# Reordering the first loads and two output steps of a windowed-attention and SwiGLU kernel

## The chip, the cores and the metric

The kernel runs on one core of a Trainium2 chip. The metric is the device time of one execution in microseconds (us). Before the change the median of three runs is 244.04 us (243.81 to 244.27). The profile is of one execution, whose span from the first to the last instruction is 240.8 us, at a mean granted tensor-engine clock of 0.998 of full speed.

## The reference

Attention with a causal window of 128 tokens and 4 "sink" tokens that every query may see, over 4 batches, 8 heads, 768 tokens and a head size of 64; its output, as 3072 tokens of 512 features, goes through a SwiGLU block with 1536 hidden features. Inputs and outputs are float32.

```python
scores = scale * np.matmul(q, k.transpose(0, 1, 3, 2))
keep = is_sink | in_window              # window: 0 <= query - key < 128
a = softmax(np.where(keep, scores, -1e9))
attn = np.matmul(a, v)                  # [B, H, S, D]
x = attn.transpose(0, 2, 1, 3).reshape(B * S, H * D)
g, val = x @ w_gate, x @ w_val
out = (g * sigmoid(g) * val) @ w_out
```

## The kernel before

The 3072 tokens are cut into 12 groups of 256 (three for each batch) for the attention, and into 8 blocks of 256 or 512 tokens (`SIZES`) for the SwiGLU block. Block 0, 1 and 2 are groups 0, 1 and 2; block 3 holds groups 3 and 4. Groups 1 and 2 get their keys and queries by `load_rows` and are transposed on TensorE (`step_T`); from group 3 on they come by `load_nat` and are transposed by a DMA (`xbar`). All loads of keys, queries, values and weights are issued by GpSimd (they cast float32 to bfloat16 on the way), in the order of the program:

```python
FCH = [2, 2, 2, 2, 4]          # chunks of the gate and value weights, in columns of 128

def load_gate(i):
    f0, n = sum(FCH[:i]) * P, FCH[i] * P
    for lst, w, nm in ((wgs, moe_w_gate, "wg"), (wvs, moe_w_val, "wv")):
        t = wpool.tile([P, DMC, n], BF16, tag=f"{nm}{i}", name=nm)
        nc.gpsimd.dma_start(t, w[:, f0:f0 + n].rearrange("(c p) f -> p c f", p=P))
        lst.append(t)
# [...]
load_rows(1)
load_v(0)
load_gate(0)
load_v(1)
load_gate(1)
load_gate(2)
nc.gpsimd.tensor_copy(out=vcf[64:128], in_=vcf[0:64])
load_gate(3)
load_rows(2)
load_v(2)
load_gate(4)
for i in range(4):
    load_out(i)
```

After these come the loads of group 3 (`load_nat(3)`, `load_v(3)`), then those of later groups. The DMA transposes are issued by SyncE, as are the stores of the output:

```python
def xbar(g):                                       # keys and queries, group 3 on
    # [...]
            nc.sync.dma_start_transpose(
                (kTs, qTs)[i][b][:, :, t0:t0 + P], nats[g][:, i, j])

def step_X(g, j, evict="v"):                       # attention output -> xT
    # [...]
    if g not in PEX:                               # PEX = (0, 1, 2, 4)
        def sp():
            nc.sync.dma_start_transpose(xTs[tb][:, :, off:off + P], xns[g, j])
        later.append(sp)
        return
    pt = bank([P, DMC, P], BF16, "px")
    for i in range(DMC):
        nc.tensor.transpose(pt[:, i], xns[g, j][:, i * P:(i + 1) * P], ident)
    # [...]  copy to xT by ScalarE ("a"), by VectorE at once ("now"), or later
```

One unit of the SwiGLU block is a `gate` (two matmul groups pg and pv, with a tanh, and two VectorE operations after them) or a `down` (12 matmuls pd, a scaling on ScalarE and a store). Attention steps are woven into the units: a gate runs them between pg and pv, a down spreads them over its matmuls. What a step leaves to VectorE or SyncE goes to `later` and is emitted by `flush`.

```python
us = [g0[0], g0[1], g0[2], g1[0], g1[1],           # units 0 to 4
      g1[2], g0[3], g1[3], g0[4], g1[4], g0[5], g1[5],   # 5 to 11
      *g2, *downs(0), *downs(1), *downs(2)]        # 12 to 17, then 18 to 23
weave(us, slots(
    (0, [K(1)]), (1, PVs(1)[:2] + [...]),
    (2, [A(step_X, 1, 0, "a"), A(step_X, 1, 1, "a")]),
    ((4, 4, 5, 5), T(2)), ((6, 7), Ss(2)), (6, [K(2)]),
    ((8, 8, 9, 9), PVs(2)), (11, [A(step_X, 2, 0, "now"), A(step_X, 2, 1, "now")]),
    # [...]  loads and DMA transposes of groups 3 to 7
    ((17, 18), Ss(3)), # [...]
    ((19, 19, 20, 20), PVs(3)), (21, Xs(3)),
    ((19, 20), Ss(4)), (19, [K(4)]),
    ((21, 21, 22, 22), PVs(4)), (22, Xs(4))))
```

`g0[i]` is the gate of block 0 that uses weight columns 2i and 2i + 1. `T` transposes keys and queries, `Ss` makes scores and their exponentials, `K` those of the sink tokens, `PVs` multiplies with the values and normalises (xn), `Xs` transposes xn into xT, the input of the gates. The units of block 3 come after unit 23.

Of the kernel before, what the change touches and what calls it, by code (L numbers as in the profile page):

```python
# [14 lines left out]
def kernel(  # L15
# [29 lines left out]
    PEX = (0, 1, 2, 4)  # L45

    VS = 72
    FCH = [2, 2, 2, 2, 4]
    FOF = [(i, f - sum(FCH[:i])) for i in range(len(FCH))
           for f in range(sum(FCH[:i]), sum(FCH[:i + 1]))]  # L50
    scale = 1.0 / float(D) ** 0.5
# [32 lines left out]
    def by_rows(src, b, w, pairs, t0):  # L84

        hs = slice(2 * pairs.start + w, 2 * pairs.stop, 2)
        return src[b, hs, t0:t0 + 256].rearrange("p (m r) d -> m p (r d)", r=4)
# [3 lines left out]
    def new_rows(g):  # L91
        rows[g] = rowp.tile([P, 2, NP2, 4 * D], BF16, tag="rows", name="rows")
        return rows[g]

    def load_rows(g, pairs=ALL, tensors=(0, 1)):
        b, c = divmod(g, GC)
        x = rows[g] if g in rows else new_rows(g)
        for i in tensors:
            for w in range(2):
                nc.gpsimd.dma_start(  # L100
                    x[64 * w:64 * (w + 1), i, pairs],
                    by_rows((k, q)[i], b, w, pairs, c * 256))
# [12 lines left out]
    def load_v(g):  # L115
        b, c = divmod(g, GC)
        va = vpool.tile([P, 2, H, VS], BF16, tag=f"va{g}", name="va")
        nc.vector.memset(va[:, :, :, D:D + 1], 1.0)
        for j in range(2):
            t0 = c * 256 + j * P  # L120
            nc.gpsimd.dma_start(  # L121
                va[:, j, :, 0:D], v[b, :, t0:t0 + P].rearrange("h p d -> p h d"))
        vas[g] = va

    wgs, wvs, wos = [], [], []

    def load_gate(i):
        f0, n = sum(FCH[:i]) * P, FCH[i] * P
        for lst, w, nm in ((wgs, moe_w_gate, "wg"), (wvs, moe_w_val, "wv")):
            t = wpool.tile([P, DMC, n], BF16, tag=f"{nm}{i}", name=nm)  # L130
            nc.gpsimd.dma_start(
                t, w[:, f0:f0 + n].rearrange("(c p) f -> p c f", p=P))
            lst.append(t)

    def load_out(i):
        n = DFC // 4
        t = wpool.tile([P, n, DM], BF16, tag=f"wo{i}", name="wo")
        nc.gpsimd.dma_start(
            t, moe_w_out[i * n * P:(i + 1) * n * P].rearrange("(c p) f -> p c f", p=P))
        wos.append(t)  # L140
# [47 lines left out]
    load_rows(1)  # L188
    load_v(0)
    load_gate(0)  # L190
    load_v(1)
    load_gate(1)
    load_gate(2)
    nc.gpsimd.tensor_copy(out=vcf[64:128], in_=vcf[0:64])
    load_gate(3)
    load_rows(2)
    load_v(2)
    load_gate(4)
    for i in range(4):
        load_out(i)  # L200

# [264 lines left out]
    def A(fn, *a):  # L466
        return lambda: fn(*a)

    def T(g):
        return [A(step_T, g, i, p2) for p2 in range(2) for i in range(2)]  # L470

    def Ss(g):
        return [A(step_S, g, p2) for p2 in range(2)]

    def PVs(g):
        return [A(step_PV, g, j, hh) for hh in range(2) for j in range(2)]

    def Xs(g):
        return [A(step_X, g, j) for j in range(2)]

    def K(g):
        return A(step_K, g)
# [109 lines left out]
    def L(*fs):  # L592
        def f():
            for x in fs:
                x()
        return f
# [2 lines left out]
        (0, [K(1)]), (1, PVs(1)[:2] + [A(step_PV, 1, 0, 1, "a"), A(step_PV, 1, 1, 1, "a"), flush]),  # L599
        (2, [A(step_X, 1, 0, "a"), A(step_X, 1, 1, "a")]),  # L600
        ((4, 4, 5, 5), T(2)), ((6, 7), Ss(2)), (6, [K(2)]),
        ((8, 8, 9, 9), PVs(2)), (11, [A(step_X, 2, 0, "now"), A(step_X, 2, 1, "now")]),
        (11, [L(A(load_nat, 4), A(load_v, 4))]),
        (12, [A(xbar, 3)]), (12, [L(A(load_nat, 5), A(load_v, 5))]),
        (15, [A(xbar, 4)]), (15, [L(A(load_nat, 6), A(load_v, 6))]),
        ((17, 18), Ss(3)), (18, [A(step_ks, 1)]), (18, [A(step_vsb, 1)]),
        (17, [A(xbar, 5)]), (17, [L(A(load_nat, 7), A(load_v, 7))]),
        ((19, 19, 20, 20), PVs(3)), (21, Xs(3)),
        ((19, 20), Ss(4)), (19, [K(4)]),
        ((21, 21, 22, 22), PVs(4)), (22, Xs(4))))  # L610

# [56 lines left out]
```

The softmax here doesn't subtract the row's maximum and nothing guards it: scores larger than these inputs give would overflow.

## Time and profile before

| | before |
|---|---|
| median of 3 runs | 244.04 us |
| span in the profile | 240.8 us |
| TensorE matmul busy | 230.8 us, 96% |
| VectorE busy | 159.9 us, 66% |
| ScalarE busy | 110.5 us, 46% |
| GpSimd busy | 70.6 us, 29% |
| software DMA queue (GpSimd's loads) | 13.90 MB, 72.6% of 16 engines' span |
| hardware DMA queue (SyncE, ScalarE) | 13.41 MB, 27.8% |

Busy times are shares of the whole span. PE is TensorE's matmul, PEld its weight loads, DVE is VectorE, ACT ScalarE, POOL GpSimd, SP SyncE; a q after the name is the engine's sequencer. "A <- B" in a view of waits means that A waited and B ended the wait. In the timeline a line is a row of like instructions: its start, its length, engine, line of the program, operation, what it writes and reads, how many; in brackets the idle time before it and what ended it. Matmul ends are modelled, so starts are the surer numbers. The program's line numbers are those of the kernel before: L239 is the transposing matmul of `step_T`, L254 the DMA transpose of `xbar`, L287 the scores, L383 the DMA transpose and L388 the TensorE transpose of `step_X`, L395 its VectorE copy, L418 the gate's matmuls, L449 those of `down`.

### The profile page before, as it was taken

The page shows a single profiled execution, that of the slowest core. Times are in us where ns is not written, and L with a number is a line of the kernel's source. Part 1 is how long each engine was busy: PE and PEld are TensorE (multiplying, and loading weights), DVE is VectorE, ACT ScalarE, POOL GpSimd, SP SyncE. Part 2 cuts the span into 40 slices and gives each one's busy share as a digit, 9 for nine tenths or more (in the row PEclk, how much of TensorE's full clock was granted, in tenths as well). Part 3 has the DMA queues.
Part 4 walks back from the last instruction along what each step waited for, and adds up shares of the span by engine and source line. Part 5 has one row for each costly group of instructions (what it writes and reads, how often), then busy time and mean ns, then how long its engine had stood idle before and what let it go on. Part 6 is the DMA issues. An engine that isn't in the chain of part 4 may idle for free.

```text
span 240.8 us, 5000 instructions
## 1 busy us (share of the span) xinstructions
PE 230.8 (96%) x1951; PEld 131.3 (55%) x1975; DVE 159.9 (66%) x340; ACT 110.5 (46%) x223; POOL 70.6 (29%) x92
## 2 busy tenths in 40 slices
PE   7979899999999999999999999999999999999994
PEld 2648778886444445454445444445444445488443
DVE  5797579978663598970597991488971498877100
ACT  4886265236641655511656512556612662232112
POOL 8975744705926209600082600000000000000000
PEclk9999999999999999999999999999999999999999
DMA  7999999999999999995799957550204200200132
GB/s 127 177 185 196 187 207 195 156 155 118 147 136 259 209 165 126 141 66 156 110 145 119 134 41 133 129 132 4 44 0 133 87 0 3 44 0 3 44 131 87
DMA packets 105638, 27.87 MB, mean 116 GB/s; under 512 B 92688, under 2 KB 102672, under 8 KB 105616
## 3 DMA queue, kind: packets, MB, share of 16 engines
q0 software_dynamic: 72512, 13.90, 72.6%
q1 hardware_dynamic: 32576, 13.41, 27.8%
q8 instruction: 15, 0.25, 0.4%
q10 hardware_dynamic: 528, 0.26, 0.4%
q14 instruction: 7, 0.06, 0.1%
HBM read 28.34 MB, written 6.29 MB: 144 GB/s over the span
## 4 chain that ended last, share of the span: by engine, by line
PE 77%; DMA 10%; DVE 6%; POOL 4%; issue 1%; ACT 1%; DVEq 0%; POOLq 0%
PE pd L449 24%; PE pv L418 23%; PE pg L418 22%; PE s L287 4%; DMA rows<-in_q_dram 3%; DMA wv<-in_moe_w_val_dram 3%; PE o L350 3%; DMA xT<-xn 3%; DVE ht L432 2%; POOL va L121 1%; DVE u L431 1%; DVE xn L364 1%; POOL rows L100 1%; DVE e L299 1%; POOL x L187 1%
## 5 line engine op out<-in xcount | busy, mean ns | idle before, releaser
L418 PE MATMUL pg<-xT,wg 128*128 128x256 bf16 (+1 forms) x379 | 73.7, 325 | 2.4 <-DMA wg<-in_moe_w_gate_dram 0.8
L425 ACT ACTIVATE th<-pg 128x512 f32<-128x512 f32 x72 | 43.3, 602 | 70.3 <-PE pg L418 68.1
L418 PE MATMUL pv<-xT,wv 128*128 128x256 bf16 (+1 forms) x374 | 73.5, 325 | 0.8 <-DVE xn L364 0.2
L431 DVE SCALAR_TENSOR_TENSOR u<-th,pg 128x512 bf16<-128x512 f32 x72 | 49.1, 682 | 34.4 <-ACT th L425 34.4
L449 PE MATMUL pd<-wo,ht 128*128 128x512 bf16 (+1 forms) x291 | 65.2, 370 | 0.6 <-issue 0.2
L432 DVE TENSOR_TENSOR ht<-u,pv 128x512 bf16<-128x512 bf16 x72 | 49.5, 687 | 10.9 <-PE pv L418 4.3
L418 PEld LDWEIGHTS <-wg 128*128 128x128 bf16 x384 | 37.3, 98 | 28.3 <-issue 1.6
L418 PEld LDWEIGHTS <-wv 128*128 128x128 bf16 x384 | 34.4, 98 | 19.9 <-issue 1.7
L294 ACT ACTIVATE e<-s 128x512 bf16<-128x512 f32 (+1 forms) x88 | 42.8, 578 | 3.9 <-PE s L287 3.9
L449 PEld LDWEIGHTS <-ht 128*128 128x128 bf16 x300 | 27.9, 98 | 28.5 <-issue 0.5
L453 ACT ACTIVATE ot<-pd 128x512 f32<-128x512 f32 (+1 forms) x25 | 14.6, 583 | 48.4 <-PE pd L449 46.4
L110 POOL DMA_DIRECT2D nat<-in_k_dram x18 | 15.9, 896 | 55.2 <-DMA qT<-nat 53.0
L299 DVE TENSOR_TENSOR e<-e,mask 128x1024 bf16<-128x1024 bf16 (+1 forms) x44 | 26.9, 648 | 3.6 <-ACT e L294 3.6
L121 POOL DMA_DIRECT2D va<-in_v_dram x24 | 21.6, 925 | 3.2 <-DMA wo<-in_moe_w_out_dram 2.0
L364 DVE TENSOR_TENSOR xn<-o,rcp 128x256 bf16<-128x256 f32 x46 | 19.5, 424 | 1.6
L350 PEld LDWEIGHTS <-e 128*128 128x128 bf16 x352 | 15.4, 98 | 8.2
L350 PE MATMUL o<-va,e 128*128 128x65 bf16 x352 | 17.4, 193 | 0.1
L110 POOL DMA_DIRECT2D nat<-in_q_dram x18 | 16.0, 908 | 2.6 <-DMA wv<-in_moe_w_val_dram 1.6
L287 PE MATMUL s<-qT,kT 64*128 64x128 bf16 (+1 forms) x240 | 13.1, 237 | 0.0
L358 DVE RECIPROCAL rcp<-o 128x4 f32<-128x4 f32 x48 | 8.3, 175 | 6.6 <-PE o L350 6.4
L287 PEld LDWEIGHTS <-kT 64*128 64x128 bf16 x240 | 7.7, 94 | 7.3 <-issue 6.3
L239 PE MATMUL pt<-ident,rows 64*64 64x64 bf16 x128 | 4.8, 243 | 0.8 <-DMA rows<-in_q_dram 0.7
(62 smaller groups left out, 77.3 us busy)
## 6 DMA issues: line engine op xcount, KB each, us to landing
out_dram<-ot SPq DMA_DIRECT2D x23, 256.0 KB
va<-in_v_dram POOLq DMA_DIRECT2D x24, 128.0 KB, 6.8
nat<-in_k_dram POOLq DMA_DIRECT2D x18, 128.0 KB, 5.7
nat<-in_q_dram POOLq DMA_DIRECT2D x18, 128.0 KB, 5.9
wo<-in_moe_w_out_dram POOLq DMA_DIRECT2D x4, 384.0 KB, 11.7
wg<-in_moe_w_gate_dram POOLq DMA_DIRECT2D x4, 256.0 KB, 8.1
wv<-in_moe_w_val_dram POOLq DMA_DIRECT2D x4, 256.0 KB, 8.7
rows<-in_k_dram POOLq DMA_DIRECT2D x4, 128.0 KB, 7.0
```

Of the source, the lines that this page charges most:

```text
L110: nc.gpsimd.dma_start(x[:, i, j].rearrange("p (h d) -> p h d", d=D), src[b, :, t0:t0 + P].rearrange("h p d -> p h d"))
L121: nc.gpsimd.dma_start(va[:, j, :, 0:D], v[b, :, t0:t0 + P].rearrange("h p d -> p h d"))
L287: nc.tensor.matmul(pss[2 * pp + h][:, col:col + n], kTs[b][r, p, kk:kk + P], qTs[b][r, p, qq:qq + n], start=True, stop=True)
L294: nc.scalar.activation(e_t[g][:, h0 + h, lo:512], pss[2 * pp + h][:, lo:512], AF.Exp, scale=scale)
L299: nc.vector.tensor_tensor(e, e, m[:, :, lo:512].broadcast_to([P, 2, 512 - lo]), op=ALU.mult)
L350: nc.tensor.matmul(o, l, r, start=(c == 0 and i == 0), stop=(i == len(mms) - 1), skip_group_check=True)
L364: nc.vector.tensor_tensor(xn, po[:, :, 0:D], rcp.broadcast_to([P, 4, D]), op=ALU.mult)
L418: nc.tensor.matmul(ps[:, i * n:(i + 1) * n], ws[fi][:, c, fo * P:(fo + 1) * P], x[:, c], start=(c == 0), stop=(c == DMC - 1))
L425: nc.scalar.activation(th, pg, AF.Tanh, scale=0.5)
L431: nc.vector.scalar_tensor_tensor(u, th, 1.0, pg, op0=ALU.add, op1=ALU.mult)
L432: nc.vector.tensor_tensor(hts[tb][:, f:f + two].rearrange("p a n -> p (a n)"), u, pv, op=ALU.mult)
L449: nc.tensor.matmul(po, hts[tb][:, f, ts * P:(ts + 1) * P], wos[f // n][:, f % n, lo:hi], start=(f == 0), stop=(f == DFC - 1))
```

## The change

Four things are moved, and one is cut in two. The gate weights of the second chunk are loaded ahead of group 1's values, which now stand between that chunk's two halves. Keys and queries of group 2 are loaded ahead of the fourth chunk of gate and value weights. The last chunk, of four columns of 128, becomes two of two. Of group 2's output one half is transposed a unit earlier. Group 3's value products move so that its output's DMA transposes are issued a unit earlier. Nothing is added to or taken from what is computed. The aim is that the tensor engine finds its first operands there when it comes to them.

```diff
-    FCH = [2, 2, 2, 2, 4]
+    FCH = [2] * 6
...
-    def load_gate(i):
+    def load_gate(i, which=(0, 1)):
         f0, n = sum(FCH[:i]) * P, FCH[i] * P
-        for lst, w, nm in ((wgs, moe_w_gate, "wg"), (wvs, moe_w_val, "wv")):
+        both = (wgs, moe_w_gate, "wg"), (wvs, moe_w_val, "wv")
+        for lst, w, nm in (both[x] for x in which):
...
     load_gate(0)
+    load_gate(1, (0,))
     load_v(1)
-    load_gate(1)
+    load_gate(1, (1,))
     load_gate(2)
     nc.gpsimd.tensor_copy(out=vcf[64:128], in_=vcf[0:64])
+    load_rows(2)
     load_gate(3)
-    load_rows(2)
     load_v(2)
     load_gate(4)
+    load_gate(5)
...
-        ((8, 8, 9, 9), PVs(2)), (11, [A(step_X, 2, 0, "now"), A(step_X, 2, 1, "now")]),
+        ((8, 8, 9, 9), PVs(2)),
+        ((10, 11), [A(step_X, 2, 0, "now"), A(step_X, 2, 1, "now")]),
...
-        ((19, 19, 20, 20), PVs(3)), (21, Xs(3)),
+        ((19, 19, 19, 20), PVs(3)), (20, Xs(3)),
```

## The prediction

> **What bounds the kernel now.** I read the page first. Its slices show the tensor engine (PE) at 9 tenths or more nearly everywhere and the DMA engines full for the first 18 slices of 6 us.
>
> ```profile
> PE   7979899999999999999999999999999999999994
> ...
> DMA  7999999999999999995799957550204200200132
> ```
>
> So the end is set by a PE that hardly rests, and a change that moves loads can only give back the moments in which PE waits. The view of waits, cut to PE, lists them (total, times, longest, in us):
>
> ```profile
> PE pg L418 <- DMA wg<-in_moe_w_gate_dram: 0.8, 1, 0.8
> PE pt L239 <- DMA rows<-in_q_dram: 0.7, 1, 0.7
> PE pg L418 <- DMA xT<-xn: 0.5, 1, 0.5
> ...
> PE pg L418 <- DVE xT L395: 0.5, 1, 0.5
> ```
>
> These are the four that the change can touch: 2.5 us out of 240.8, about 1%. That caps the whole matter. Next the timeline of PE shows where they lie and what is around them (start, length):
>
> ```profile
> 16.25 1.05 PE L418 MATMUL pv<-xT,wv 128*128 128x256 bf16 x8
> 18.05 1.05 PE L418 MATMUL pg<-xT,wg 128*128 128x256 bf16 x8 [0.75 <-DMA wg<-in_moe_w_gate_dram]
> ...
> 21.11 1.04 PE L418 MATMUL pg<-xT,wg 128*128 128x256 bf16 x8
> ...
> 26.51 0.83 PE L239 MATMUL pt<-ident,rows 64*64 64x64 bf16 x17
> 28.07 0.63 PE L239 MATMUL pt<-ident,rows 64*64 64x64 bf16 x15 [0.72 <-DMA rows<-in_q_dram]
> 28.63 1.05 PE L418 MATMUL pv<-xT,wv 128*128 128x256 bf16 x8
> ...
> 55.48 1.04 PE L418 MATMUL pg<-xT,wg 128*128 128x256 bf16 x8
> 56.45 0.50 PE L287 MATMUL s<-qT,kT 64*128 64x256 bf16 x8
> ```
>
> The last two lines look harmless: the scores of group 3 start without idle time. I asked for them because they are the first PE work that needs a later load: keys and queries of group 3 (nat), transposed by DMA. The sync engine's timeline gives those four transposes' issues, and the view of line 287 gives a semaphore wait of PE's sequencer:
>
> ```profile
> 42.83 1.29 SPq L254 DMA_TRANSPOSE kT<-nat  x1
> 44.63 1.19 SPq L254 DMA_TRANSPOSE qT<-nat  x1
> 45.91 1.33 SPq L254 DMA_TRANSPOSE kT<-nat  x1
> 47.34 1.29 SPq L254 DMA_TRANSPOSE qT<-nat  x1
> ```
> ```profile
> L287 PEldq EVENT_SEMAPHORE  x1: 51/51/51, 56.2 to 56.2; - x1
> ```
>
> In the trace's semaphore records these four complete at 49.6, 51.5, 53.3 and 56.1 us. PE wanted the result at 56.35. **It had 0.2 us to spare, no more.** This is what I build the prediction on.
>
> **What the Trainium skill says.** (1) "DMA: Bandwidth & Descriptors", section "Issuing engines are not separate DMA queues": transfers issued by different engines run on the same 16 DMA engines and interleave. The trace agrees: the last of those transposes needs 8.8 us (47.34 to 56.1) while values and rows of group 4 are still landing (to 57.6 by the landing times); the same kind of transpose, issued at 89.79 with no load in flight, completes at 93.0, after 3.2 us. (2) The same page, "Specifications", asks for at least 512 B for line rate. The split of the last weight chunk halves its rows to 256 bf16, which is 512 B, just at the limit. Landing times agree that little is lost: the 512-column chunks land 2.58 and 2.53 us after the one before, the 256-column ones 1.32 to 1.39 for half the bytes. (3) "Perfetto Trace Analysis", "Tensor Engine Instruction": the end of a matmul in the profile is a model. The trace agrees: groups of 8 are given 1.04 us but follow one another at 0.87. I therefore count from start to start.
>
> **The change part by part.** All landing times are issue plus time to landing, from the views of the tiles wg, wv, rows, va; in the first 48 us they follow each other without a hole, so I reorder them and add up their spacings.
>
> *A. Second gate chunk ahead of group 1's values.* Landings now: wv of chunk 0 15.50, va 15.86 and 16.63, wg of chunk 1 18.00, then wv 19.32, wg of chunk 2 20.64. Moved forward, wg lands at 15.50 + 1.35 = 16.85 and the values at about 17.2 and 18.0. The gate starts when PE is free, 16.25 + 0.87 = 17.12, instead of 18.05: 0.9 us sooner. The values are wanted 1.1 us after that (18.2) and are there. But the next gate needs chunk 2, still 20.64; it started at 21.11, so only 21.11 - 20.65 = **0.46 us** survives. The following 0.33 us wait on the scalar engine's xT copy moves along with it.
>
> *B. Group 2's rows ahead of chunk 3.* The rows land at 25.62, 26.37, 27.06 and 28.02, about 0.8 each. Put behind chunk 2 (21.97) they are all there at 21.97 + 3.2 = 25.2. PE wants them at 26.51 - 0.46 = 26.05: no wait. The 32 transposing matmuls take 1.01 us undisturbed (30.48 to 31.49 in the next unit); they took from 26.51 to 28.63, 2.12: **1.1 us** saved. Chunk 3 then lands at about 27.9, wanted at 32.38 - 1.56 = 30.8; chunks 4 and 5 between 30 and 34.6, wanted from 35.8 and 40.6. None of them stalls.
>
> *C. The split of the last chunk.* Two more issues of 0.75 us on GpSimd, which is not waited for, and 4 x 1.33 - (2.58 + 2.53) = **0.2 us** more of DMA time ahead of everything behind it, group 3's keys included.
>
> *D. Output of group 2: one half in unit 10, one in unit 11.* In unit 10 PE is free at 43.08, but the normalised half (xn of VectorE, 43.68 + 0.42) is only there at 44.10. PE would stall 1.0 us there, where it did not before. From 44.10: transposes 0.22, pv 0.87, pg 0.87, transposes 0.22, pv 0.87 give 47.15 for gate(2), which now starts at 46.76: a **loss of 0.4 us**, though the 0.45 us wait on the copy of xT disappears. VectorE was busy without a hole from 35.20 to 46.71 and its work stays the same.
>
> So gate(2) starts 0.46 + 1.1 - 0.4 = 1.16 us sooner, and PE stands before group 3's scores at 56.45 - 1.16 = 55.3.
>
> *E. The floor.* Nothing of A to D makes nat of group 3 land sooner: the same bytes lie ahead of it in a full queue, plus 0.2 us from C. Its last transpose completes at 56.1 + 0.2 = 56.3, PE can start at about 56.5. **The whole 1.16 us is turned into a new wait, and 0 to 0.2 us is lost.**
>
> *F. Groups 3's output sooner.* The chain of waits and its continuation show it:
>
> ```profile
> 72.02 6.53 DMA xT<-xn
> 78.55 0.14 issue
> 78.68 1.02 PE pg L418 x4
> ```
>
> PE's last matmuls before it start 15 at 74.74, 0.216 apart (0.43 for two), so PE is free at 77.98 and gate(3) waits 0.7 us. The two DMA transposes go out at 70.70 and 72.02, behind the store of unit 20, which itself waits for its scalar copy (ends 70.2). With the change they stand ahead of that store, behind the one issued at 68.69: some 1.6 us sooner, landing near 76.9. xn for them is done by 67.4. PE no longer waits: **0.7 us saved**, and this one lies behind the floor, so it counts. After 80 us PE has no DMA wait left; what is gained there is kept to the end.
>
> Sum: 0 (+0.1) - 0.7 = **-0.6 us: 244.04 gives 243.4**.
>
> **Rivals.** (1) *No floor*: the transposes complete sooner than I reckon, or something in the queue empties earlier. Then A, B and D count as well: -1.16 - 0.7 = -1.9, 242.1. For it: nothing but the unclear share of 16 engines between two queues; against it: the DMA slices are full up to there. (2) *The new order makes a stall*: values of group 1 or chunk 2 late, group 3's transposes pushed by more than 0.2, or unit 19, now with three value steps, short of PSUM banks. That could cost 0.5 to 1 and eat F: 244 to 244.6. For it: several margins are under 1 us. (3) *F gives nothing*, since earlier transposes meet the loads of group 6 (landing to 78.9) and come no sooner: then about 244.1.
>
> **Range and chances.** Middle 243.4; eight times in ten between 242.3 and 244.4, which takes in F alone failing and half of rival 1. 2% is 4.9 us, twice the sum of all four waits, and no stall I can name costs that: same 0.98, faster 0.01, slower 0.01.
>
> **What would show it.** Right: PE's waits on wg and on rows gone; a new wait of PE at line 287 on DMA qT<-nat of about 1 us near 55 to 56.5; a PE wait on xn at line 388 near 42 us, of about 1 us; the L383 issues near 69 and gate(3) without a wait on xT. Wrong: group 3's scores starting well before 56 (rival 1), or after 57, or gate(3) still waiting for xT.

## The result and the profile after

The changed kernel takes 242.72 us (median of 6 runs, 241.97 to 242.97) against 244.16 us before in the same session: a ratio of 0.994, with a 95% interval of 0.9923 to 0.9957. That is 1.44 us less, where 0.6 was forecast (243.4, range 242.3 to 244.4). The profiled run of the changed kernel has a span of 240.2 us, 0.6 less than the one of before. All line numbers of the changed kernel are 1 to 3 higher: L290 is the scores, L421 the gate's matmuls, L386 and L391 the DMA and TensorE transposes of `step_X`. gate(2) and gate(3) are the first gates of blocks 2 and 3.

The view of waits of the changed kernel, cut to PE, answers to the four waits shown of before (total, times, longest, us):

```profile
PE px L391 <- DVE xn L367: 1.3, 3, 0.8
PE s L290 <- DMA qT<-nat: 1.3, 1, 1.3
```

The waits on wg, on rows, on the DMA of xT and on VectorE's copy of xT are gone from it. In their place stand two others: on xn ahead of group 2's output (0.8 of the 1.3 us; the rest was there before), and on the transposed queries of group 3. PE's timeline gives the places:

```profile
17.26 1.04 PE L421 MATMUL pg<-xT,wg 128*128 128x256 bf16 x8
...
20.56 1.05 PE L421 MATMUL pg<-xT,wg 128*128 128x256 bf16 x8
...
25.97 1.08 PE L242 MATMUL pt<-ident,rows 64*64 64x64 bf16 x32
26.99 1.05 PE L421 MATMUL pv<-xT,wv 128*128 128x256 bf16 x8
...
42.53 0.28 PE L391 MATMUL px<-ident,xn 128*128 128x128 bf16 x2 [0.82 <-DVE xn L367]
...
45.49 1.04 PE L421 MATMUL pg<-xT,wg 128*128 128x256 bf16 x8
...
54.23 1.04 PE L421 MATMUL pg<-xT,wg 128*128 128x256 bf16 x8
56.53 0.51 PE L290 MATMUL s<-qT,kT 64*128 64x256 bf16 x8 [1.26 <-DMA qT<-nat]
...
78.05 1.03 PE L421 MATMUL pg<-xT,wg 128*128 128x512 bf16 x4
```

Read it against before. The transposes of group 2 are now one row of 32, and what follows them starts at 26.99, 1.64 us sooner than 28.63. gate(2) starts at 45.49, 1.27 us sooner. Then the scores of group 3 start at 56.53, 0.08 us *later* than before: 1.27 us had been gained, and the new wait takes 1.26. Only behind it is there a gain, at gate(3): 78.05 instead of 78.68. The sync engine's timeline shows its source, group 3's output going out ahead of the store (before, the L383 row stood at 70.70):

```profile
66.63 2.10 SPq L457 DMA_DIRECT2D out_dram<-ot  x2
68.84 2.89 SPq L386 DMA_TRANSPOSE xT<-xn  x2
71.82 7.43 SPq L457 DMA_DIRECT2D out_dram<-ot  x4
```

From gate(3) to the end nothing differs: span minus start of gate(3) is 162.1 us in both kernels. It lies between 162.1 and 162.6 in all the profiles below, so the start of gate(3) tells a profiled run's story to within 0.5 us.

### The profile page after: what moved, and what is told of

It reads as the page before. It is cut to its first block, busy times and chain, and to the rows that moved or that the text cites. A ratio compares the mean times of both kernels' runs of the same rounds, so it can differ in the third digit from the quotient of the medians.

```text
span 240.2 us, 5002 instructions
## 1 busy us (share of the span) xinstructions
PE 230.8 (96%) x1951; PEld 131.9 (55%) x1975; DVE 159.6 (66%) x340; ACT 110.6 (46%) x223; POOL 72.1 (30%) x94
## 4 chain that ended last, share of the span: by engine, by line
PE 72%; DMA 18%; POOL 3%; issue 2%; DVE 1%; SPq 1%; ACT 1%; POOLq 0%; DVEq 0%
PE pd L452 26%; PE pv L421 20%; PE pg L421 19%; DMA wv<-in_moe_w_val_dram 6%; DMA nat<-in_q_dram 5%; DMA rows<-in_k_dram 4%; DMA qT<-nat 4%; PE s L290 3%; PE o L353 3%; SPq L257 1%; POOL rows L100 1%; POOL va L121 1%; POOL x L188 1%; PE o L333 1%; PE pk L318 0%
## 5 line engine op out<-in xcount | busy, mean ns | idle before, releaser
L421 PE MATMUL pv<-xT,wv 128*128 128x256 bf16 (+1 forms) x376 | 73.6, 325 | 0.7 <-DVE xn L367 0.2
L421 PE MATMUL pg<-xT,wg 128*128 128x256 bf16 (+1 forms) x377 | 73.5, 325 | 0.9 <-ACT xT L394 0.3
L421 PEld LDWEIGHTS <-wg 128*128 128x128 bf16 x384 | 37.4, 98 | 26.3 <-issue 1.2
L421 PEld LDWEIGHTS <-wv 128*128 128x128 bf16 x384 | 34.3, 98 | 19.9 <-issue 1.7
L290 PE MATMUL s<-qT,kT 64*128 64x128 bf16 (+1 forms) x240 | 13.1, 237 | 1.3 <-DMA qT<-nat 1.3
L290 PEld LDWEIGHTS <-kT 64*128 64x128 bf16 x240 | 7.7, 94 | 8.6 <-issue 7.6
L132 POOL DMA_DIRECT2D wv<-in_moe_w_val_dram x6 | 4.8, 807 | 1.0 <-DMA wv<-in_moe_w_val_dram 0.6
(62 smaller groups left out, 79.5 us busy)
```

What stands on the lines that cost most here:

```text
L290: nc.tensor.matmul(pss[2 * pp + h][:, col:col + n], kTs[b][r, p, kk:kk + P], qTs[b][r, p, qq:qq + n], start=True, stop=True)
L421: nc.tensor.matmul(ps[:, i * n:(i + 1) * n], ws[fi][:, c, fo * P:(fo + 1) * P], x[:, c], start=(c == 0), stop=(c == DMC - 1))
```

## The experiments

The first theory is the forecast's, **the floor**: whatever is gained ahead of group 3's scores is lost in waiting for their DMA transposes, and the gain is the wait removed on xT. The rival: **the loads count too**, since 1.44 us is more than the 0.6 of one pair of profiles. The first four ran beside 49 runs of the kernel before (median 244.04).

**e1, group 3's output alone.**

```diff
 (kernel before)
-        ((19, 19, 20, 20), PVs(3)), (21, Xs(3)),
+        ((19, 19, 19, 20), PVs(3)), (20, Xs(3)),
```

> The kernel before with one edit: group 3's value products and its output's transposes a unit sooner, no load moved. Floor theory (all that is gained before group 3's scores is lost in the wait for their DMA transposes; the gain is the removed wait on xT): the wait of PE on xT near 78 us is gone and the time falls by 0.7 us or, if the unprofiled runs wait longer there than the profiled one, up to 1.4. Rival (the loads count too, about half of the 1.4 us): 0.7 us at most.

Measured: 243.16 us, ratio 0.9963 (0.9950 to 0.9977), 0.9 us faster. The size fits the floor theory, but its profile does not fit the picture: the wait on xT is not gone. Waits of PE:

```profile
PE s L287 <- DMA qT<-nat: 1.2, 1, 1.2
...
PE pg L418 <- DMA xT<-xn: 0.8, 1, 0.8
...
PE pt L239 <- DMA rows<-in_q_dram: 0.3, 1, 0.3
PE pg L418 <- DMA wg<-in_moe_w_gate_dram: 0.3, 1, 0.3
```

No load was moved here, yet in this profile the early loads cost PE 0.6 us and not 1.5, and the floor took it back: 1.25 us at the scores, as in the changed kernel. The xT transposes were issued at 70.1 and 71.4 and completed at 78.3 and 79.3. Two things are suggested: the early waits differ from run to run and the floor evens them out, and there is a second floor at gate(3), which a sooner issue lowers but need not remove.

**e2, the loads alone.**

```diff
 (changed kernel)
-        ((10, 11), [A(step_X, 2, 0, "now"), A(step_X, 2, 1, "now")]),
+        (11, [A(step_X, 2, 0, "now"), A(step_X, 2, 1, "now")]),
-        ((19, 19, 19, 20), PVs(3)), (20, Xs(3)),
+        ((19, 19, 20, 20), PVs(3)), (21, Xs(3)),
```

> The kernel before with the load order and the split of the last chunk alone; the output steps stay where they were. Floor theory: the waits on wg and rows are gone, PE reaches group 3's scores 1.5 us sooner (55.0) and waits there until 56.4; the time is that of before, within 0.3 us, and gate(3) still waits for xT. Rival (the loads count): 0.7 us or more faster.

Measured: 243.48 us, ratio 0.9983 (0.9967 to 1.0000), 0.4 us faster, with an interval from 0.8 to nothing. That lies between the two theories. The profile has the wait at the scores as forecast, 1.84 us:

```profile
56.94 0.51 PE L290 MATMUL s<-qT,kT 64*128 64x256 bf16 x8 [1.84 <-DMA qT<-nat]
...
80.04 1.03 PE L421 MATMUL pg<-xT,wg 128*128 128x512 bf16 x4
```

It doesn't show the wait on xT, because PE came late to gate(3): by the trace's clock records TensorE had half its clock from 57.73 to 61.14 us (0.62 on average from 57 to 60). That costs 3.41 x 0.5 = 1.7 us, an estimate. Without it PE would have come at 78.3, ahead of the last xT transpose, which completed at 78.7 in this run: about 0.5 us of waiting, as the floor theory has it.

**e3, both outputs of group 2 back in unit 11.**

```diff
 (changed kernel)
-        ((10, 11), [A(step_X, 2, 0, "now"), A(step_X, 2, 1, "now")]),
+        (11, [A(step_X, 2, 0, "now"), A(step_X, 2, 1, "now")]),
```

> The changed kernel with both output transposes of group 2 back in unit 11. Floor theory: the stall of 0.8 us on xn near 42 us is gone, PE gains 0.4 us there and waits 0.4 us longer at group 3's scores (1.7 instead of 1.3): the time equals that of the changed kernel within 0.3 us. Rival: 0.4 us faster than the changed kernel.

Measured: 242.82 us, ratio 0.995 (0.9930 to 0.9971): the changed kernel's 0.994 within either interval. The 0.8 us stall on xn is gone, gate(2) starts at 45.23 instead of 45.49, and the wait at the scores is 2.11 us instead of 1.26, as the transposes completed at 57.0 in this run. The step does nothing measurable for the time as long as the floor stands behind it.

**e4, keys and queries of group 3 ahead of the output weights.**

```diff
 (changed kernel)
+    load_nat(3)
     for i in range(4):
         load_out(i)
 ...
-    load_nat(3)
     load_v(3)
```

> The changed kernel with group 3's keys and queries loaded ahead of the output weights, which lowers the floor: nat lands near 39 instead of 46 us, its transposes are done well before 55, the output weights land near 46 instead of 42, wanted at 57. Floor theory: the 1.26 us wait at group 3's scores is gone and the time falls by about 1.2 us below the changed kernel, less what gate(3) then waits for xT if that does not come sooner as well. Rival (no floor in the unprofiled runs): same as the changed kernel.

Measured: 245.99 us, ratio 1.0084 (1.0052 to 1.0115), 2 us **slower**. The step forecast did happen: the transposes were done at 51.1 and the scores of group 3 started at 55.33 without a wait. But the next scores, of group 4, were hit; PE's timeline (the scores are L291 here) and the page's row of the granted clock, in tenths, 6.1 us to a digit:

```profile
62.70 0.23 PE L291 MATMUL s<-qT,kT 64*128 64x128 bf16 x2 [0.54 <-DMA qT<-nat]
66.04 0.93 PE L291 MATMUL s<-qT,kT 64*128 64x256 bf16 x10 [3.11 <-DMA qT<-nat]
```
```profile
PEclk9999999999889999999999999999999999999999
```

Group 4's transposes completed at 59.9 to 66.0, where they are done between 57.7 and 59.2 in the changed kernel. The last one's 6.8 us have two parts in the trace. It was issued 3.3 us later (58.30 instead of 55.04), since group 4's own keys and queries landed 2 to 5 us later: ahead of them the output weights landed 2.3 to 3.3 us apart, beside group 3's transposes, where they had landed 1.9 to 2.1 apart. And it took 7.7 us from issue instead of 4.2. With two buffers for nat, the end of group 3's transposes is what lets the loads of group 5 start, and ending them 5.3 us sooner let those start at 51.6 instead of 57.0, on top of group 4's transposes. The floor had moved from one group to the next.

The waiting is not all of the loss. After it TensorE had half its clock from 65.74 to 69.15 us, another 1.7 us by the estimate of e2. Six of the seven runs had a mean clock of 0.986 to 0.993; the seventh, at full clock, took 244.57 us, half a microsecond more than before.

The next four, and e11, lower the floor the other way, by clearing the DMA engines around group 3's transposes. The four ran beside 14 runs of before (median 243.98). The theory is now **two floors**: one at the scores near 56, one at gate(3) near 78.

**e5, values of group 4 behind the keys and queries of group 5.**

```diff
 (changed kernel)
-        (11, [L(A(load_nat, 4), A(load_v, 4))]),
+        (11, [A(load_nat, 4)]),
-        [...] (12, [L(A(load_nat, 5), A(load_v, 5))]),
+        [...] (12, [L(A(load_nat, 5), A(load_v, 4), A(load_v, 5))]),
```

> The changed kernel with the values of group 4 loaded after the keys and queries of group 5 (which wait until group 3's transposes are done), so that 2 of the 6 loads that share the DMA engines with those transposes are gone. They should complete 1 to 2 us sooner than 55.9. Two-floor theory (PE is held first by group 3's transposes near 56, then by group 3's output near 78): the 1.26 us wait at group 3's scores mostly goes, but the output of group 3 lands near 77.5 and gives back all but 0.3 us: 0.2 to 0.5 us faster than the changed kernel. Rival with one floor only: 1.2 us faster.

Measured: 242.14 us, ratio 0.992 (0.9899 to 0.9941), about 0.5 us below the changed kernel by the ratios, though the intervals overlap. The wait has moved from one floor to the other:

```profile
55.46 0.51 PE L290 MATMUL s<-qT,kT 64*128 64x256 bf16 x8 [0.16 <-DMA qT<-nat]
...
78.48 1.02 PE L421 MATMUL pg<-xT,wg 128*128 128x512 bf16 x4 [1.32 <-DMA xT<-xn]
```

Here 1.26 us at the scores have become 0.16, and gate(3), which did not wait, waits 1.32.

**e6, the same edit in the kernel before.**

> The same edit in the kernel before. There PE comes to group 3's scores when the transposes are just done, so freeing the DMA engines is worth little: same as before within 0.3 us (two-floor theory: group 3's output still holds gate(3) near 78). Rival (the transposes hold PE in the unprofiled runs of the kernel before as well): 0.5 to 1 us faster than before.

Measured: 243.16 us, ratio 0.9962 (0.9947 to 0.9976), 0.9 us faster. I expected nothing, so this missed. Its profile has no wait at the scores and one of 1.5 us on xT, and gate(3) starts at 79.37. The size fits the rival, that the transposes hold PE in usual runs of the kernel before as well, as they did in e1's profile; but this profile does not show where the 0.9 us is gained.

**e7, e5 with both outputs of group 2 in unit 11.** Its edits are those of e3 and e5 together.

> As e5, and both output transposes of group 2 back in unit 11, so that PE reaches group 3's scores another 0.4 us sooner. Two-floor theory: as e5 within 0.3 us, with a longer wait on xT at gate(3). One floor: 0.4 us faster than e5.

Measured: 241.88 us, ratio 0.9906 (0.9882 to 0.9931), 0.3 us below e5, which the intervals do not separate; gate(3) waits 0.9 us on xT.

**e8, both floors lowered.**

```diff
 (e7)
-    PEX = (0, 1, 2, 4)
+    PEX = (0, 1, 2, 3, 4)
```

> As e7, and group 3's output is transposed by TensorE instead of by DMA: 8 matmuls of 0.055 us more (0.44 us) on PE, and no wait on xT by DMA is left at gate(3). Two-floor theory: with both floors lowered the loads count at last: PE reaches gate(3) near 76.5 to 77 instead of 78.05, and the time is 1.0 to 1.5 us below the changed kernel, near 241.5. One-floor theory: 0.4 us slower than e7, for the added matmuls.

Measured: **241.53 us, ratio 0.9895 (0.9877 to 0.9914)**, the lowest median of all, 1.1 us below the changed kernel by the ratios. Below e7 it is 0.3 us, which the intervals do not separate. gate(3) starts at 77.32 without a wait, although PE does 8 transposes more:

```profile
55.34 0.51 PE L290 MATMUL s<-qT,kT 64*128 64x256 bf16 x8 [0.25 <-DMA qT<-nat]
...
64.97 0.39 PE L391 MATMUL px<-ident,xn 128*128 128x128 bf16 x4
...
65.84 0.39 PE L391 MATMUL px<-ident,xn 128*128 128x128 bf16 x4
...
77.32 1.03 PE L421 MATMUL pg<-xT,wg 128*128 128x512 bf16 x4
```

**e11, the same floors with the old loads.** The edits of e5 and e8 in the kernel before: what are the loads worth when nothing behind them waits?

> The kernel before with both floors lowered as in e8 (values of group 4 later, group 3's output transposed by TensorE) and its old load order. Two-floor theory: now the waits on wg and rows count in full, so it is 1.2 to 1.6 us slower than e8, some 1.0 us faster than the kernel before. Rival (the loads are worth 0.4 us whatever the floors): 0.4 to 0.6 us slower than e8.

Measured: 242.89 us, ratio 0.995 (0.9931 to 0.9968), beside 17 runs of before (median 244.23). Against e8's 0.9895 that is 0.0055 x 244 = 1.3 us, with 0.7 to 2.0 from the two intervals. Its profile has the loads' waits in full, and none behind them:

```profile
PE pg L418 <- DMA wg<-in_moe_w_gate_dram: 1.0, 1, 1.0
PE pt L239 <- DMA rows<-in_q_dram: 0.6, 2, 0.4
```

So the new load order is worth 0.4 us (0 to 0.8) in the kernel as it was (e2) and 1.3 us with both floors lowered. This is what a floor means, and it speaks for the floors, though the two ranges nearly touch. That there are two is shown by the traces more than by the times: in e5 and e7 PE waits 1.3 and 0.9 us at gate(3) once the first floor is lowered, and in e8 it no longer does. (e8 also has group 3's output a unit earlier; that part was not tried apart.)

**e9, e10 and e12, the two kernels profiled again**, unchanged.

> The kernel before once more, for a second profile. If the wait at group 3's scores is the usual state and its absence in the first profile an accident: a wait on the transposes of 0.3 to 1.3 us at the scores, with the loads' own waits near 18 and 28 us smaller by as much. If the first profile is typical: no wait at the scores, waits on wg and rows of 0.7 to 0.8 us.

> The changed kernel once more, for a second profile: no waits on wg and rows, the transposes complete at 55.9 to 56.7 and PE waits there 1 to 2 us; gate(3) starts between 78 and 79.

> The kernel before, a third profile. The two profiled runs so far (242.56 and 243.59 us) are faster than its median, so a usual run must wait longer somewhere before gate(3). Either at group 3's scores (a transpose completing at 57 or later, as in the second profile of the changed kernel) or on xT at gate(3) (over 1.3 us).

Waits of PE in the repeats, beside the others (us; "transposes" is when the last of group 3's completes, the sixteenth and last update of its semaphore):

| profile | time | early loads (wg, wv, rows) | transposes | wait at scores | wait on xT | gate(3) starts |
|---|---|---|---|---|---|---|
| before | 242.56 | 1.5 | 56.2 | 0 | 0.5 | 78.68 |
| before, e9 | 243.59 | 1.0 | 56.2 | 0 | 1.3 | 79.28 |
| before, e12 | 243.54 | 0.9 | 56.5 | 0.6 | 0.8 | 79.17 |
| e1 (loads of before) | 243.29 | 0.6 | 56.8 | 1.2 | 0.8 | 79.41 |
| changed | 241.97 | 0 | 56.4 | 1.3 | 0 | 78.05 |
| changed, e10 | 243.28 | 0.7 | 57.7 | 2.2 | 0 | 79.37 |

Both kernels differ from themselves by as much as from each other, and in e10 the changed kernel reaches gate(3) later than in any profile of before. What the change is worth is therefore read from the times of many runs, and from profiles only where the time is spent. In the rows with the loads of before, a smaller early wait tends to come back at the scores or at gate(3).

The forecasts for the repeats mostly missed. e9 has no wait at the scores, but less early waiting than the first profile, and its 1.3 us on xT was in neither case named. In e10 the transposes complete a microsecond late, and PE waits 0.7 us on wg and wv. e12 found 0.6 us at the scores, with the transposes at 56.5 and not 57, and no run late at gate(3).

## Why the prediction was right, and where its sizes were off

- **A and B, the loads: right, with too little to spare.** Forecast 17.12 and 20.65 for the first two gates, measured 17.26 and 20.56; 1.56 us gained behind group 2's transposes, measured 1.64. But in six of the other seven profiles with the new order PE waits 0.2 to 0.3 us on wg of the third chunk, and in e7 and e10 also 0.5 and 0.4 us on wv of the second, which lands no sooner than before (19.2 and 19.3 in the first two profiles) and which the forecast did not reckon.
- **C, the split: right in size, without effect.** The last two chunks land between 29.13 and 34.48, 5.35 us, where the one large chunk took 5.11 (29.22 to 34.33): 0.24 us more, forecast 0.2. Group 3's transposes complete 0.2 us later than in the first profile of before (56.4 and 56.2), as forecast, but they differ more than that between profiles of one kernel.
- **D, output of group 2: right.** A stall of 0.82 us (forecast 1.0), gate(2) 1.27 us sooner (forecast 1.16). e3 shows that taking it back changes nothing while the floor stands.
- **E, the floor: the mechanism right, its height not as firm as stated.** Scores at 56.53, forecast "about 56.5"; wait 1.26. The completions that the forecast read from the semaphore records, 49.6 to 56.1, are each the eleventh of a transpose's sixteen updates; the sixteenth stand at 49.9, 52.1, 53.5 and 56.2, which leaves 0.2 us to spare all the same. (The transpose issued at 89.79 was not quite alone either: a load followed at 89.96.) But "the whole 1.16 us is turned into a new wait" was a reading of one profile. e2 puts the loads' worth at 0.4 us, with the forecast's 0 just at the edge of its interval (0 to 0.8).
- **F, group 3's output: the mechanism right, its size too small, its margin too large.** The issues moved from 70.70 to 68.84, about as forecast, but the last transpose completed at 77.8 and not at 76.9: issued 1.6 us sooner, it was done 0.7 us sooner. PE arrived at 78.05, so the margin was 0.25 us. And the wait to be won was taken as 0.7 from one profile, whereas the repeats of before show 0.8 and 1.3. e1 alone measures 0.9 us (0.6 to 1.2), though its one profile still shows a wait on xT.

The forecast 0.6 us lies outside the measured interval (1.05 to 1.9); its range held because it allowed for half of rival 1. That the first two profiles differ by just 0.6 us at gate(3) is luck, as their repeats show. The sum fell short by these two terms: 0.9 from F and 0.4 from the loads make 1.3, and 1.44 was measured. Rival 1 of the forecast, no floor at all, would have been 1.9 us, at the end of that interval; the wait in the profile, and e2 with e11, speak against it, not the time. Rival 2's stall from a crowded unit 19 did not come, but a small one on wv did (e7, e10). Rival 3 was half true: the earlier transposes gained less than half of their head start while the values of group 6 were landing (to 79.5), and in e1's profile gate(3) still waited.

Open: none of the three profiled runs of before is as slow as its median. At 244.04 us gate(3) should start near 80, and the latest seen is 79.28. Where the usual run spends the rest, and so where e6 found its 0.9 us, the profiles do not show. One hint: in e11's profile PE came to the scores only at 57.09, without a wait there, 0.6 us later than in the first profile of before, whose early loads it shares. So some of it may lie in the early loads.

## What to carry to other kernels

When a load order is improved, look for the next thing behind it that is timed by the DMA queue and not by the engine that was waiting: the engine's arrival less its completion time, as they are before, is all that the improvement can earn. A wait of no length in the profile, as the scores at 56.45 with 0.2 us to spare, can be the most important one. And a gain read as the wait in one profile is a sample: profile the same kernel twice before a wait of 0.5 us is taken as a size.

## What was not expected of the hardware

A DMA transpose within the chip's memory took several times as long beside loads: the fourth of group 3's took 8.6 us in the changed kernel (issued at 47.76, complete at 56.39), and 2.5 us was enough in the kernel before for one issued at 88.48, behind others too, between one group's loads (landed by 88.52) and the next (issued from 89.96). Starting it sooner beside loads gains less than the head start: in e4 the fourth was issued 7.1 us sooner than in the changed kernel and completed 5.3 us sooner, and group 4's then completed up to 6.8 us later. Taking the 2 loads of group 4's values out of the way (e5, e6) brought group 3's last one forward by 1.1 and 1.0 us, the low end of the 1 to 2 expected.

A transpose updates its semaphore sixteen times, and the engine waits for the last: in the eight profiles in which PE waits 0.1 us or more at group 3's scores, it starts 0.13 to 0.14 us after the sixteenth. For group 3's last transpose in e12 the eleventh came 0.7 us before the sixteenth, as much as the effects studied here.

Twice a wait of PE went with a halved TensorE clock of 3.41 us, which costs more than many of the waits: in e2's profile, beside a wait of 1.84 us, and in e4's, beside one of 3.11 us. After waits of 2.11 us (e3) and 2.24 us (e10) the clock stayed full. A mean clock of 0.993 or less is found in 6 of 7 runs of e4, 3 of 22 of e2, 1 of 11 of e3 and 3 of the 49 of before beside them. What sets it off is not shown.
